# Spreading the shift products of an adaptive-norm attention kernel, with its first input tracked in token halves

## The chip, the cores and the metric

The kernel runs on one core of one Trainium2 chip. The metric is the device time of one execution in microseconds (us), median of several runs. For each run the span of the core's work (about 1.8 us less than the time, in most runs) and the mean granted TensorE clock are known too.

## The reference, cut to what matters

```
mod = silu(c) @ w_mod -> sa, ca, ga, sb, cb, gb          # six rows of 1024
h   = layernorm(x) * (1 + ca) + sa                       # x: 2048 x 1024
q   = h @ wq                                             # 32 heads of 128
p   = softmax(q @ k.T / sqrt(128)); o = p @ v            # 512 keys, 4 key groups
x   = x + ga * (o @ wo)
h   = layernorm(x) * (1 + cb) + sb
x   = x + gb * ((silu(h @ w_gate) * (h @ w_up)) @ w_down)
```

All in bf16 with f32 accumulation. The change touches only the start: the first `h`, the first eight heads of `q` for tokens 0 to 511, and the first iterations of attention.

## The kernel before

Tokens go in chunks of 512. The kernel does not wait for the shift `sa`: it projects the first eight heads from the scaled input alone ("raw" queries), and adds the shift's contribution, `sa @ wq`, later, as a column of 128 numbers a head. These columns are the *shift products*: 8 matmuls of one column for each head. `T.op` records who reads and writes each buffer and sets the semaphore waits; a buffer is one record, whatever part of it is used. `PB[b]` is the record of PSUM bank `b`.

```python
def x_gain(hf):                      # gain columns 1 + ca, four at a time
    V.tensor_copy(mod_bf[:, jt:jt + HK], psap(XB * 512, [[2, HK]]))      # PSUM -> bf16
    mod_gain(0, hf * HK, HK, B_modc, B_g[0])                             # + 1, bf16
    A.activation(gain_f[...], gain[0][...], AF.Copy)                     # f32 copy for ACT

def x_mod(hf, c0, n):                # scale tokens c0 .. c0+n of four chunks of the input
    for dt in (0, 2, 1, 3):
        ...                          # DVE for chunks 0, 1; ACT for chunks 2, 3
        ... writes=[PB[dt // 2], B_hT[0][dt]]      # one record for both token halves

for kc in range(HK):                 # first token half, heads 0 to 2
    for h in range(3):
        q_first(h, kc, 0, 2 * P)     # reads B_hT[0][kc]
    if kc == 2:
        x_first(tl, 0, HK)           # transposes of tile 3
        x_mod(0, 2 * P, 2 * P)       # second token half
        norm_last(512, 512)
for k in range(4): mod_ca(1, k)
for kc in range(HK):
    for h in range(3): q_first(h, kc, 2 * P, 2 * P)
x_first(2, HK, HK); x_first(tl, HK, HK)
for k in range(4, DT): mod_ca(1, k)
x_gain(1); x_mod(1, 0, CH)
...
def q_bias_mm(h0, h1):               # shift products of heads h0 .. h1-1
    for h in range(h0, h1):
        for kc in range(DT):
            mm(bank(BB, 1, 2 * h), wq_s[sl][...], mod_bf[:, kc:kc + 1], ..., PB[BB])  # BB = SCB + 3
    V.tensor_copy(bq[:, h0:h1], psap(BB * 512 + 2 * h0, ...))
...
for i in range(1, NA + 2):           # one attention head an iteration
    if i % 4 == 1 and i > 1: load_wq((i + 3) // 4 + 1)   # 1 MB of query weights
    if 2 <= i < NQ0: q_shifted(i)
    ...
    if i in LOADO: load_wo(LOADO[i])                     # 1 MB of output weights
    if 2 <= i < 1 + Hkv:
        k_turn(i - 1, XB); V.tensor_copy(kd, ks)         # one key group through bank XB
    ...
    if i == 1: scores(0); q_bias_mm(2, NQ0)              # 48 products
    if i > NQ0: qproj(i + LEAD)
    elif i % 2 == 0: qproj(NQ0 - 1 + i // 2)             # heads 8, 9, 10 at i = 2, 4, 6
    ...
    if 1 <= i - 1 < NA: scores(i - 1)
    if 0 <= i - 2 < NA: pv(i - 2)
```

The loads that matter here are all issued by one engine (SP), in program order: ..., query weights of group 2, the second token chunk of `x` (1 MB), keys of groups 1 to 3, values.

The softmax here doesn't subtract the row's maximum and nothing guards it: scores larger than these inputs give would overflow.

## Time and profile before

| | value |
|---|---|
| median of the three runs known at the start | 1278.52 us (1278.47 to 1280.67) |
| the profiled run: time, span, mean granted clock | 1281.05 us, 1279.3 us, 0.997 |
| PE busy; chain of waits on PE | 99%; 98% |

These are the page's busy line and the chain line of the kernel before. PE is the whole story: a gain has to come out of PE's gaps or its clock.

```profile
PE 1262.2 (99%) x7542; PEld 646.7 (51%) x7684; DVE 479.9 (38%) x896; ACT 341.8 (27%) x390; POOL 42.0 (3%) x102
...
PE 98%; issue 1%; ACT 0%; DVE 0%; POOL 0%; POOLq 0%; ACTq 0%
```

The next lines are from the timeline of PE in the kernel before: start, duration, line, operation, output and input, count, and in brackets PE's idle time before it with what ended it. Line 268 is the helper that issues every matmul, 272 the one for transposes; `128x1` are the one-column products.

```profile
start us, us, engine line op out<-in xcount [idle before <-releaser]
...
13.75 0.50 PE L268 MATMUL ps<-arena 128*128 128x256 bf16 x3 [1.07 <-ACT arena L492]
...
18.03 5.34 PE L268 MATMUL ps<-arena 128*128 128x512 bf16 x24 [0.35 <-DVE arena L489]
...
33.67 1.42 PE L268 MATMUL ps<-mod_bf,arena 128*128 128x1 bf16 x48 [1.80 <-ACT arena L755]
34.95 0.59 PE L272 MATMUL ps<-arena 128*128 128x128 bf16 x4
35.76 5.89 PE L268 MATMUL ps<-arena 128*128 128x512 bf16 x27 [0.22 <-DVE bq L663]
```

Three things are to be seen. At 13.75 PE had waited 1.07 us for a write by ACT. At 33.67 it had waited 1.80 us for ACT's exponentials, for the 48 shift products write a bank that the scores also use. And the stretch of 27 matmuls that begins with head 8's projection, at 35.76, took 5.89 us, far too long for its work. The windows view of the same kernel tells why: the third number from the end of a line, after the engines' busy times, is the clock granted to PE (here 0.89, 0.50, 0.93).

```profile
core 0: us, PE busy (x) PEld busy (x) DVE busy (x) ACT busy (x) POOL busy (x), PEclk, DMA share, GB/s
30.00:35.00 5.00, 3.14 (x57) 1.80 (x56) 3.14 (x11) 2.64 (x3) 0.00 (x0) 0.89 1.06 303
35.00:40.00 5.00, 4.78 (x18) 1.99 (x16) 1.68 (x4) 0.16 (x1) 0.00 (x0) 0.50 0.15 57
40.00:45.00 5.00, 4.95 (x51) 3.43 (x51) 2.80 (x8) 3.93 (x4) 0.00 (x0) 0.93 0.13 26
```

### The profile page before, as it was taken

The page shows a single profiled execution, that of the slowest core. Times are in us where ns is not written, and L with a number is a line of the kernel's source. Part 1 is how long each engine was busy: PE and PEld are TensorE (multiplying, and loading weights), DVE is VectorE, ACT ScalarE, POOL GpSimd, SP SyncE. Part 2 cuts the span into 40 slices and gives each one's busy share as a digit, 9 for nine tenths or more (in the row PEclk, how much of TensorE's full clock was granted, in tenths as well). Part 3 has the DMA queues.
Part 4 walks back from the last instruction along what each step waited for, and adds up shares of the span by engine and source line. Part 5 has one row for each costly group of instructions (what it writes and reads, how often), then busy time and mean ns, then how long its engine had stood idle before and what let it go on. Part 6 is the DMA issues. An engine that isn't in the chain of part 4 may idle for free.

```text
span 1279.3 us, 17804 instructions
## 1 busy us (share of the span) xinstructions
PE 1262.2 (99%) x7542; PEld 646.7 (51%) x7684; DVE 479.9 (38%) x896; ACT 341.8 (27%) x390; POOL 42.0 (3%) x102
## 2 busy tenths in 40 slices
PE   8999999999999999999999999999999999999999
PEld 4565545655445664455654444444444444444444
DVE  4555324765237652265322321233222331221222
ACT  3555303555015550055520111011100111011100
POOL 1021000000000010000000000000000000000000
PEclk9899999999999999999999999999999999999999
DMA  9799402967008841054352974046421654035200
GB/s 325 202 237 263 104 1 68 203 138 161 9 19 179 163 104 42 1 128 116 71 148 75 282 236 132 18 146 166 134 73 41 199 147 132 17 115 165 66 9 25
DMA packets 235854, 155.31 MB, mean 121 GB/s; under 512 B 129024, under 2 KB 222080, under 8 KB 235776
## 3 DMA queue, kind: packets, MB, share of 16 engines
q1 hardware_dynamic: 177520, 95.45, 31.2%
q10 hardware_dynamic: 58256, 58.73, 14.5%
q8 instruction: 60, 0.98, 0.3%
q14 instruction: 18, 0.15, 0.0%
HBM read 119.54 MB, written 4.19 MB: 97 GB/s over the span
## 4 chain that ended last, share of the span: by engine, by line
PE 98%; issue 1%; ACT 0%; DVE 0%; POOL 0%; POOLq 0%; ACTq 0%
PE ps L268 98%; ACT arena L755 0%; PE ps L272 0%; ACT arena L492 0%; DVE arena L489 0%; DVE rl L773 0%; DVE arena L668 0%; POOL arena L296 0%; DVE tmp L795 0%; DVE arena L797 0%; DVE gain L462 0%; DVE mod_bf L477 0%; DVE bq L663 0%; POOL arena L291 0%; POOL arena L290 0%
## 5 line engine op out<-in xcount | busy, mean ns | idle before, releaser
L268 PE MATMUL ps<-arena 128*128 128x512 bf16 (+2 forms) x7237 | 1254.2, 333 | 12.3 <-POOL arena L407 2.2
L268 PEld LDWEIGHTS ps<-arena 128*128 128x128 bf16 x7379 | 636.3, 98 | 623.4 <-issue 5.5
L755 ACT ACTIVATE arena<-ps 128x1024 bf16<-128x1024 f32 x256 | 261.8, 1023 | 354.5 <-PE ps L268 342.7
L986 ACT ACTIVATE arena<-ps 128x512 bf16<-128x512 f32 x112 | 66.9, 597 | 506.4 <-PE ps L268 506.4
L987 DVE TENSOR_TENSOR arena<-ps,arena 128x512 bf16<-128x512 f32 x112 | 77.4, 691 | 276.3 <-PE ps L268 276.3
L795 DVE TENSOR_TENSOR tmp<-ps,rowb 128x512 f32<-128x512 f32 (+1 forms) x65 | 44.4, 683 | 319.1 <-PE ps L268 319.1
L642 DVE CAST arena<-ps 128x512 bf16<-128x512 f32 x120 | 83.0, 691 | 54.9 <-PE ps L268 54.9
L776 DVE TENSOR_TENSOR arena<-ps,rl 128x512 bf16<-128x512 f32 x128 | 88.5, 691 | 4.8 <-DVE rl L773 0.4
L773 DVE RECIPROCAL rl<-ps 128x4 f32<-128x4 f32 x128 | 23.3, 182 | 119.2 <-PE ps L268 119.2
L414 DVE BATCH_NORM_STATS2 st<-x_res 128x6 f32<-128x512 bf16 x62 | 42.3, 683 | 3.5 <-DMA x_res<-in_A_x_dram 3.4
L419 POOL TENSOR_SCALAR rstd<-mv 128x1 f32<-128x1 f32 x28 | 6.3, 226 | 893.8 <-DVE mv L418 893.8
L587 DVE SCALAR_TENSOR_TENSOR arena<-arena 128x1024 bf16<-128x1024 bf16 x24 | 29.2, 1215 | 0.0
L797 DVE TENSOR_TENSOR arena<-tmp,x_res 128x512 bf16<-128x512 f32 (+1 forms) x33 | 22.3, 676 | 1.1
L797 DVE TENSOR_TENSOR x_res<-tmp,x_res 128x512 bf16<-128x512 f32 x32 | 22.1, 692 | 1.1
L430 DVE TENSOR_SCALAR arena<-arena,gain,mod_bf 128x512 bf16<-128x512 bf16 x56 | 20.3, 405 | 0.0
L425 DVE TENSOR_SCALAR nsc<-x_res,mv,rstd 128x1024 bf16<-128x1024 bf16 x30 | 16.0, 534 | 0.0
L421 POOL TENSOR_TENSOR rstd<-rstd,mhalf 128x1 f32<-128x1 f32 x28 | 15.8, 563 | 2.3
L602 POOL TENSOR_SCALAR arena<-arena,c 128x128 bf16<-128x128 bf16 x24 | 14.4, 616 | 32.7 <-PE ps L268 32.4
L268 PEld LDWEIGHTS ps<-sc_bf,arena 128*128 128x128 bf16 x192 | 6.7, 96 | 2.3
L268 PE MATMUL ps<-sc_bf,arena 128*128 128x1 bf16 x192 | 6.8, 163 | 0.1
L418 DVE BATCH_NORM_AGGREGATE mv<-st 128x2 f32<-128x12 f32 x28 | 5.8, 209 | 1.0
L655 DVE COPY arena<-ps 128x512 f32<-128x512 f32 x4 | 2.7, 689 | 7.9 <-PE ps L268 7.9
(53 smaller groups left out, 50.9 us busy)
## 6 DMA issues: line engine op xcount, KB each, us to landing
arena<-in_A_wq_dram SPq DMA_DIRECT2D x31, 1024.0 KB, 6.0
arena<-in_B_w_gate_dram ACTq DMA_DIRECT2D x28, 1024.0 KB, 5.4
arena<-in_B_w_up_dram ACTq DMA_DIRECT2D x28, 1024.0 KB, 8.3
arena<-in_A_wo_dram SPq DMA_DIRECT2D x8, 1024.0 KB, 7.8
arena<-in_B_w_down_dram SPq DMA_DIRECT2D x7, 1024.0 KB, 8.5
out_dram<-arena SPq DMA_DIRECT2D x15, 256.0 KB, 2.0
x_res<-in_A_x_dram SPq DMA_DIRECT2D x3, 1024.0 KB, 7.8
arena<-in_w_mod_dram SPq DMA_DIRECT2D x8, 256.0 KB, 6.0
```

The source lines that it names most:

```text
L268: T.op(PE, lambda: TE.matmul(out_ap, lhsT, rhs, start=start, stop=stop, skip_group_check=skip), reads=reads, writes=[bank_buf])
L414: T.op(DVE, lambda: V.bn_stats(st_[sl][:, hf * 6:hf * 6 + 6], x_res[:, t, hf * 512:hf * 512 + 512]), reads=[B_x[t]], writes=[B_st[sl]])
L430: T.op(DVE, lambda: V.tensor_scalar(dst[:, dt, :], dst[:, dt, :], gain[gi][:, dt:dt + 1], mod_bf[:, ccol + dt:ccol + dt + 1], op0=ALU.mult ...
L587: T.op(DVE, lambda: V.scalar_tensor_tensor(mt[n % 2], mt[n % 2], 1.0, sc_row, op0=ALU.mult, op1=ALU.mult, accum_out=mcol[:, n:n + 1]), rea ...
L642: T.op(DVE, lambda: V.tensor_copy(qT_s[qs], bank(b)), writes=[PB[b], B_qT[qs]])
L755: T.op(ACT, lambda: A.activation(ex_s[es][:, 2 * kp:2 * kp + 2, :], banks2(SCB + 2 * kp), AF.Exp, scale=att_scale), writes=[PB[SCB + 2 * k ...
L773: T.op(DVE, lambda: V.reciprocal(rl[r][:, :].rearrange("p (a b) -> p a b", a=2), psap(PVB * 512 + P, [[512, 2], [130, 2]])), writes=both + ...
L776: T.op(DVE, lambda: V.tensor_tensor(o_s[os_].rearrange("p (a b) d -> p a b d", a=2), psap(PVB * 512, [[512, 2], [130, 2], [1, P]]), rlb, A ...
L795: T.op(DVE, lambda: V.tensor_tensor(tmp[s][:, 0:n], bank(b, n), rowb[ri][:, c0:c0 + n], ALU.mult), reads=[B_row[ri]], writes=[PB[b], B_tmp ...
L797: T.op(DVE, lambda: V.tensor_tensor(dst[:, c0:c0 + n], tmp[s][:, 0:n], x_res[:, t, c0:c0 + n], ALU.add), reads=[B_tmp[s], B_x[t]], writes= ...
L986: T.op(ACT, lambda: A.activation(sg_s[ss], bank(gb), AF.Silu), writes=[PB[gb], B_sg[ss]])
L987: T.op(DVE, lambda: V.tensor_tensor(guT[:, ft, :], bank(ub), sg_s[ss], ALU.mult), reads=[B_sg[ss]], writes=[PB[ub], B_gu[ft]])
```

## The change

The intent is to start the first projections and head 8's projection earlier: (1) the two token halves of the first input get records of their own, and the second gain columns are prepared sooner; (2) the gain is read from PSUM once, as f32, for both engines; one warm-up matmul goes; (3) the shift products are made 16 at a time in iterations one, three and five, into the query bank, which nothing else uses then; (4) key groups 2 and 3 are both turned in iteration three; (5) the load of the query weights of heads 12 to 15 moves from iteration five to six, since their slot is read by the last shift products. Cut to its core:

```diff
 def x_gain(hf):
-    tensor_copy(mod_bf[...], psap(XB * 512, [[2, HK]])); mod_gain(0, ...)
-    A.activation(gain_f[...], gain[0][...], AF.Copy)
+    V.tensor_scalar(gain_f[:, hf * HK:(hf + 1) * HK], psap(XB * 512, [[2, HK]]), 1.0, None, op0=ALU.add)
-def x_mod(hf, c0, n):                       # ... writes B_hT[0][dt]
+def x_mod(hf, c0, n, bufs):                 # ... writes bufs[dt]
 ...
-                if k % 2 == 1:
+                if k == 5:
                     warm(1, WB)
 ...
-                    x_mod(0, 2 * P, 2 * P)
+                    x_mod(0, 2 * P, 2 * P, B_hB)
 ...
+            x_first(2, HK, HK)
             for kc in range(HK):
                 for h in range(3):
-                    q_first(h, kc, 2 * P, 2 * P)
-            x_first(2, HK, HK)
-            x_first(tl, HK, HK)
-            for k in range(4, DT):
-                mod_ca(1, k)
-            x_gain(1)
-            x_mod(1, 0, CH)
+                    q_first(h, kc, 2 * P, 2 * P, B_hB)
+                if kc == 1:
+                    x_first(tl, HK, HK)
+                    for k in range(4, DT):
+                        mod_ca(1, k)
+                    x_gain(1)
+                    x_mod(1, 0, CH, B_hT[0])
 ...
-                if i % 4 == 1 and i > 1:
+                if i % 4 == 1 and i > 5 or i == 6:
                     load_wq((i + 3) // 4 + 1)
 ...
-                if 2 <= i < 1 + Hkv:
-                    k_turn(i - 1, XB)
+                for gk in {2: (1,), 3: (2, 3)}.get(i, ()):
+                    k_turn(gk, XB)
 ...
                     if i == 1:
                         scores(0)
-                        q_bias_mm(2, NQ0)
+                    if i in (1, 3, 5):
+                        q_bias_mm(i + 1, i + 3, QB)
```

More of the change, by code (lines that the diff above doesn't have):

```diff
@@ L458, in mod_mm, with mod_gain @@
                        k == 0 and n == 0, k == DT - 1, [wbuf, B_sc], PB[XB], skip=True)
-            def mod_gain(gi, d0, n, cbuf, gbuf):
-                jt = (1 + 3 * gi) * DT + d0
-                T.op(DVE, lambda: V.tensor_scalar(gain[gi][:, d0:d0 + n], mod_bf[:, jt:jt + n], 1.0, None, op0=ALU.add),
+            def mod_gain(gi, cbuf, gbuf):
+                jt = (1 + 3 * gi) * DT
+                T.op(DVE, lambda: V.tensor_scalar(gain[gi][:, :], mod_bf[:, jt:jt + DT], 1.0, None, op0=ALU.add),
                      reads=[cbuf], writes=[gbuf])
@@ L475, in x_gain @@
             def x_gain(hf):
-                jt = DT + hf * HK
-                T.op(DVE, lambda: V.tensor_copy(mod_bf[:, jt:jt + HK], psap(XB * 512, [[2, HK]])), writes=[PB[XB], B_modc])
-                mod_gain(0, hf * HK, HK, B_modc, B_g[0])
-                T.op(ACT, lambda: A.activation(gain_f[:, hf * HK:(hf + 1) * HK], gain[0][:, hf * HK:(hf + 1) * HK], AF.Copy),
-                     reads=[B_g[0]], writes=[B_gf])
-            def x_mod(hf, c0, n):
+                T.op(DVE, lambda: V.tensor_scalar(gain_f[:, hf * HK:(hf + 1) * HK], psap(XB * 512, [[2, HK]]), 1.0, None, op0=ALU.add),
+                     writes=[PB[XB], B_g[0]])
+            def x_mod(hf, c0, n, bufs):
                 for dt in (0, 2, 1, 3):
@@ L488, in x_mod @@
                     if dt % 4 < 2:
-                        T.op(DVE, lambda: V.tensor_scalar(dst, src, gain[0][:, dt:dt + 1], None, op0=ALU.mult),
-                             reads=[B_g[0]], writes=[PB[dt // 2], B_hT[0][dt]])
+                        T.op(DVE, lambda: V.tensor_scalar(dst, src, gain_f[:, dt:dt + 1], None, op0=ALU.mult),
+                             reads=[B_g[0]], writes=[PB[dt // 2], bufs[dt]])
                     else:
                         T.op(ACT, lambda: A.activation(dst, src, AF.Copy, scale=gain_f[:, dt:dt + 1]),
-                             reads=[B_gf], writes=[PB[dt // 2], B_hT[0][dt]])
+                             reads=[B_g[0]], writes=[PB[dt // 2], bufs[dt]])
             MCOLS = [(j, j) for j in range(DT)]
@@ L553, in _ @@
             x_gain(0)
-            x_mod(0, 0, 2 * P)
+            x_mod(0, 0, 2 * P, B_hT[0])
             norm_last(0, 512)
@@ L655, in q_raw, with q_bias_mm @@
                     T.op(DVE, lambda: V.tensor_copy(qf[h], bank(QB0[h])), writes=[PB[QB0[h]], B_qf[h]])
-            def q_bias_mm(h0, h1):
+            def q_bias_mm(h0, h1, BB):
                 for h in range(h0, h1):
@@ L685, in k_evac, with q_first @@
                 return (kT_sb[:, gk * KT:(gk + 1) * KT, :], bank_bf(b)[:, 0:KT * P].rearrange("p (a b) -> p a b", a=KT))
-            def q_first(h, kc, c0, n):
+            B_hB = [_Buf("hB%d" % dt) for dt in range(DT)]
+            def q_first(h, kc, c0, n, bufs=B_hT[0]):
                 mm(bank(QB0[h], n, c0), wq_s[0][:, kc, h * P:(h + 1) * P], hT[0][:, kc, c0:c0 + n],
-                   kc == 0 and c0 == 0, kc == DT - 1, [B_wq[0][kc // HK], B_hT[0][kc]], PB[QB0[h]], skip=True)
+                   kc == 0 and c0 == 0, kc == DT - 1, [B_wq[0][kc // HK], bufs[kc]], PB[QB0[h]], skip=True)
             for kc in range(HK):
@@ L716, in _ @@
                 q_raw(h)
+            T.op(DVE, lambda: V.tensor_copy(gain[0][:, :], gain_f[:, :]), writes=[B_g[0]])
             qproj_mm(4, QB0[4], 0, DT)
@@ L733, in _ @@
             qproj_mm(7, QB0[7], 0, HK)
-            q_bias_mm(0, 2)
+            q_bias_mm(0, 2, BB)
             q_shifted(0)
@@ L848, in _ @@
                     load_wo(LOADO[i])
-                if 2 <= i < 1 + Hkv:
-                    k_turn(i - 1, XB)
-                    kd, ks = k_evac(i - 1, XB)
-                    T.op(DVE, lambda: V.tensor_copy(kd, ks), writes=[PB[XB], B_kT[i - 1]])
-                    if i == Hkv:
+                for gk in {2: (1,), 3: (2, 3)}.get(i, ()):
+                    k_turn(gk, XB)
+                    kd, ks = k_evac(gk, XB)
+                    T.op(DVE, lambda: V.tensor_copy(kd, ks), writes=[PB[XB], B_kT[gk]])
+                    if gk == Hkv - 1:
                         for b_ in B_hT[1]:
@@ L887, in _ @@
                         if g0 == 1:
-                            mod_gain(1, 0, DT, B_late[2], B_g[1])
+                            mod_gain(1, B_late[2], B_g[1])
                         elif g0 == 2:
```

## The prediction

> **What bounds the kernel.** TensorE. The page gives PE 1262.2 us busy of a 1279.3 us span (99%), and the chain of waits is 98% PE. From 60 us to the end I find almost no PE wait, and the diff changes nothing there. All that can be won lies in the first 55 us, where the timeline shows four PE gaps: 10.75-11.3, 12.7-13.75, 17.7-18.03 and, largest, 31.9-33.67. So this is a change of a microsecond or two.
>
> **Front (to 21 us).** In the timeline PE waits 1.07 us, until 13.75, for an ACT write of the second token half (12.72 + 2 x 0.49): chunk 3 of the first half is held by a record shared by both halves. Separate records let it run at about 12.6. The second half's and tile 3's transposes and the gain columns then move up: the gain read, at 17.00 before, comes at about 15.15 (the last gain weights land at 14.1, the DMA view), one DVE op of 0.16 us instead of DVE 0.16 + DVE 0.17 + ACT 0.20 with gaps. Chunks 4 to 7 start at 16.6 rather than 18.03: 1.4 us gained. The weights they need land at 15.6 and 18.6, and the shift weights at 21.2, 0.3 us before their new use, so I expect no new wait. Dropping one warm matmul and the ACT copy of the gain before 11.3 gains nothing: there PE waits for query weights that land at 11.1-11.3.
>
> **Shift products.** Before, 48 one-column products (1.42 us) write a score bank and so wait 1.80 us for the two exponentials (ACT 31.47-33.61); the first full projection starts at 35.76. After, 16 products (0.48 us) go to the query bank without waiting. Then the transposes of key group 1 wait for keys that land at about 32.25 (issued 23.03, 9.2 us to landing), so the projection starts near 32.7: 3.1 us earlier in all. Part is given back: in iteration three two key groups turn through one bank, the second waiting for a DVE copy that queues behind reciprocal, scaling and a query shift (0.2 + 0.7 + 0.5 + 0.4 us). PE should stand about 1.3 us at 36.6-37.9, and 16 products follow (0.48). The last 16, in iteration five, fill the 0.46 us wait for ACT seen at 48.35, so cost nothing. Walked through in order with these durations, PE ends 1.3 us ahead at iteration six, and keeps that.
>
> **Clock.** The windows view shows a granted clock of 0.50 from 33.9 to 40.6 us: twelve 512-column matmuls start 0.43 us apart instead of 0.216, a loss of some 2.4 us. The Trainium skill (TensorE: Matmul & The Clock Gate, Part 1) says a free-running window of about 3.4 us of low activity halves the clock; this trace agrees (6.7 us, two windows). As the phase is free, not every run need pay: 1280.67 and the profiled 1281.05 against 1278.47 and 1278.52 differ by just that, so I take the median before to be an unpaid run. The new gaps (about 1.45 and 1.3 us) are shorter than 1.8 us, so I expect the half clock more rarely, perhaps never.
>
> **Time.** 1278.5 - 1.3 = 1277.2 us; range 1275.0 to 1279.0. Faster by over 2%: 0.005, within 2%: 0.99, slower: 0.005.
>
> **Would show it right.** The gain read at about 15.2; first projection after the scores at 32-33; PE wait for keys, then a wait of about 1.3 us for the DVE key copy; no wait at iteration five; clock 1.00 between 30 and 45 us; runs closer together.
>
> **Would make it wrong.** The new gaps trip the half clock (up to 2 us back); shift weights landing later than planned; the unpaid runs before were partly paid (then 1275 is possible).

## The result

| | before | after |
|---|---|---|
| median, runs | 1279.27 us, 4 (1278.47 to 1280.67) | 1280.25 us, 4 (1279.87 to 1281.39) |
| ratio after over before | | 1.0008, 95% interval 0.9991 to 1.0025 |
| profiled run: span, clock | 1279.3 us, 0.997 | 1277.5 us, 1.000 |

1280.25 us lies outside the predicted 1275.0 to 1279.0 and nothing of the 1.3 us is seen. (Three of the four runs after also have 2.3 us outside the span instead of the usual 1.8; that half microsecond lies outside the core's work.)

One trap lies in the table. The two profiled spans differ by 1.8 us in favour of the change, but the one before ran partly at half clock and the one after did not. They can't be compared as they stand.

The busy line and the chain line of the changed kernel, which answer to those of before: the chain is now 96% PE, the rest being SP's issues and two loads.

```profile
PE 1259.3 (99%) x7541; PEld 646.0 (51%) x7683; DVE 480.1 (38%) x897; ACT 341.8 (27%) x388; POOL 42.2 (3%) x102
...
PE 96%; SPq 2%; DMA 1%; issue 1%; DVE 0%; ACT 0%
```

PE's timeline in the changed kernel, columns as before:

```profile
12.86 0.49 PE L268 MATMUL ps<-arena 128*128 128x256 bf16 x3
...
15.09 6.86 PE L268 MATMUL ps<-arena 128*128 128x256 bf16 x33
...
30.29 0.54 PE L268 MATMUL ps<-mod_bf,arena 128*128 128x1 bf16 x16
33.07 0.40 PE L272 MATMUL ps<-arena 128*128 128x128 bf16 x4 [2.24 <-DMA arena<-in_A_k_cache_dram]
33.30 3.66 PE L268 MATMUL ps<-arena 128*128 128x512 bf16 x27
36.80 0.39 PE L272 MATMUL ps<-arena 128*128 128x128 bf16 x4
38.78 0.38 PE L272 MATMUL ps<-arena 128*128 128x128 bf16 x4 [1.59 <-DVE arena L853]
...
50.57 0.94 PE L268 MATMUL ps<-sc_bf,arena 128*128 128x1 bf16 x32
...
57.52 1.90 PE L268 MATMUL ps<-arena 128*128 128x512 bf16 x7 [0.71 <-DMA arena<-in_A_wq_dram]
59.25 0.34 PE L268 MATMUL ps<-sc_bf,arena 128*128 128x1 bf16 x8
```

The front went as predicted: no wait at 12.86, chunks 4 to 7 within the run of matmuls that starts at 15.09, the shift products at 30.29 unhindered. Then PE stands 2.24 us for the keys of group 1 and 1.59 us between the two key turns of iteration three, and, not predicted at all, 0.71 us for query weights at 57.52. (The lines at 50.57 and 59.25 serve as marks below.) The windows of the changed kernel show a full clock in this run:

```profile
30.00:35.00 5.00, 2.71 (x30) 1.57 (x29) 2.83 (x11) 2.05 (x2) 0.00 (x0) 1.00 0.99 262
35.00:40.00 5.00, 3.33 (x47) 2.45 (x47) 2.87 (x7) 2.05 (x2) 0.00 (x0) 1.00 0.45 148
40.00:45.00 5.00, 5.00 (x60) 3.42 (x59) 2.09 (x5) 3.43 (x4) 0.00 (x0) 1.00 0.79 238
```

The chain of waits of the changed kernel, from 18.94 us on (start, duration, what), names the owners of the three waits:

```profile
18.94 4.01 SPq L299
...
22.99 10.04 DMA arena<-in_A_k_cache_dram
...
37.00 0.19 DVE rl L774
...
37.22 0.69 DVE arena L777
37.91 0.39 DVE arena L665
38.30 0.34 DVE arena L853
...
49.51 7.96 DMA arena<-in_A_wq_dram
```

The keys (issued at 22.99) landed 10.04 us later, behind the 4.01 us issue of 1 MB of `x` (line 299). The copy that frees the bank (line 853) queued behind the reciprocal (774), the scaling (777) and a query shift (665). The query weights issued at 49.51 took 7.96 us.

### The profile page after: what moved, and what is told of

Its sections match the earlier page's. It is cut to its first block, busy times and chain, and to the rows that moved or that the text cites. A ratio compares the mean times of both kernels' runs of the same rounds, so it can differ in the third digit from the quotient of the medians.

```text
span 1277.5 us, 17800 instructions
## 1 busy us (share of the span) xinstructions
PE 1259.3 (99%) x7541; PEld 646.0 (51%) x7683; DVE 480.1 (38%) x897; ACT 341.8 (27%) x388; POOL 42.2 (3%) x102
## 4 chain that ended last, share of the span: by engine, by line
PE 96%; SPq 2%; DMA 1%; issue 1%; DVE 0%; ACT 0%
PE ps L268 96%; DMA arena<-in_A_k_cache_dram 1%; DMA arena<-in_A_wq_dram 1%; SPq L331 0%; SPq L299 0%; SPq L354 0%; SPq L384 0%; SPq L363 0%; SPq L306 0%; SPq L358 0%; ACT arena L756 0%; DVE rl L774 0%; PE ps L272 0%; SPq L389 0%; DVE arena L777 0%
## 5 line engine op out<-in xcount | busy, mean ns | idle before, releaser
L599 POOL TENSOR_SCALAR arena<-arena,c 128x128 bf16<-128x128 bf16 x24 | 14.4, 618 | 32.7 <-PE ps L268 32.4
L272 PE MATMUL ps<-arena 128*128 128x128 bf16 x32 | 3.1, 218 | 3.8 <-DMA arena<-in_A_k_cache_dram 2.2
```

## The experiments

**Theory A**: the three waits are new or newly bare, and each ate a part of the gain. **Theory B**: the half clock decides; both kernels have runs with and without it, and this hides or makes the difference. **Theory C** (for two runs): the front's gain is lost somewhere later in any case. In what follows "at full clock" means runs whose mean granted clock is shown as 1.000. All kernels gave correct results. The kernels came five rounds each, beside nine runs of the kernel before.

| kernel | spans at clock 1.000, us | spans below 1.000, us | median time (before) |
|---|---|---|---|
| before, 32 runs in all | 1276.7 to 1277.1 (16 runs) | 1278.0 to 1279.8 (16) | |
| changed, first job | 1277.5, 1277.7 | 1278.6, 1279.1 | 1280.25 (1279.27) |
| changed, again | 1276.4, 1276.6, 1277.2 | 1278.4, 1278.9 | 1279.09 (1278.66) |
| keys_early | 1276.2, 1276.6, 1276.6 | 1278.4, 1278.4 | 1278.47 (1278.66) |
| wq3_first | 1275.8, 1275.8 | 1277.4, 1277.6, 1277.7 | 1279.31 (1278.66) |
| turns_spread | 1275.9, 1275.9 | 1276.6, 1277.0, 1277.7 | 1278.49 (1278.66) |
| front_only | 1275.1, 1275.2, 1275.2, 1275.4 | 1276.5 | 1277.11 (1279.91) |
| bias_only | 1278.0, 1278.1, 1278.7 | 1279.8, 1279.8 | 1280.48 (1279.91) |
| before_filled | 1277.4, 1277.4, 1277.5, 1277.5, 1277.7 | none | 1279.28 (1279.91) |
| after_filled | 1277.4, 1277.9, 1278.3, 1278.8, 1279.0 | none | 1280.12 (1278.90) |
| front_filled | 1275.0, 1275.6, 1275.6, 1276.1, 1276.4 | none | 1278.04 (1278.90) |
| all_three | 1273.5, 1273.7, 1273.7, 1273.7, 1274.0 | none | 1275.57 (1278.90) |
| three_filled | 1273.4, 1273.4, 1273.6, 1273.6, 1274.3 | none | 1275.81 (1278.90) |

### after_again: the changed kernel, unedited

> The changed kernel again, unedited, for a baseline on this chip with more rounds. Theory A (new waits ate the gain: keys landing at 33.0 us, the second key turn's 1.6 us wait for a DVE copy, the 0.7 us wait for the query weights of heads 12 to 15 at 57.5 us): ratio to the kernel before 1.000 to 1.001, the same three PE waits within 0.3 us. Theory B (the half clock decides: runs of either kernel fall on two levels about 2 us apart, by the phase of the clock's window): a ratio that moves with how many runs of each show a clock below 1.000.

Measured: ratio 1.0001 (0.9989 to 1.0014); waits of 2.1, 1.6 and 0.8 us. At full clock its runs are within half a microsecond of those of before, so the gain is missing at full clock as well: theory B can't be the whole cause. But two of five runs fall to the lower level, as three of the nine of before do, so the change does not spare the half clock either.

### before_again: the kernel before, against itself

> The kernel before against itself, for the spread and, if its profile falls at a clock of 1.000, for its own walk through the first 60 us without the half clock. Expected: ratio 1.000 within 0.001; spans of 1276.7 to 1277.1 at clock 1.000, of 1278.5 to 1279.8 below it; at full clock head 8's projection starts at 35.5 to 35.8 us and iteration seven's gate products at 50.7 to 50.9.

Measured: ratio 0.9996, three of five runs at full clock, the profiled one among them, so its timeline is the fair counterpart of the changed kernel's:

```profile
33.71 1.35 PE L268 MATMUL ps<-mod_bf,arena 128*128 128x1 bf16 x48 [1.80 <-ACT arena L755]
34.93 0.38 PE L272 MATMUL ps<-arena 128*128 128x128 bf16 x4
35.36 3.44 PE L268 MATMUL ps<-arena 128*128 128x512 bf16 x27
...
50.67 0.94 PE L268 MATMUL ps<-sc_bf,arena 128*128 128x1 bf16 x32
...
58.47 0.34 PE L268 MATMUL ps<-sc_bf,arena 128*128 128x1 bf16 x8
```

The same wait of 1.80 us is there, without the half clock. Head 8's projection starts at 35.36 (a little before the 35.5 to 35.8 that I expected), not at 35.76, and its stretch of 27 matmuls takes 3.44 us, not 5.89: the half clock cost 2.45 us there. It had also slowed the products and the key turn before that by 0.4 us, which the prediction booked as gain of the change. 50.67 and 58.47 (the gate products of iterations seven and nine) serve as marks below.

### front_only and bias_only: each half of the change alone

```diff
 # front_only: parts 1 and 2 of the change; products, key turns, loads as before
 # bias_only: parts 3, 4 and 5; the front as before
```

> The kernel before with the front part of the change alone (split records of the token halves, gain columns read once, one warm matmul less); shift products, key turns and weight loads as before. Theory A (the two parts don't add: the keys' landing at 33 us takes what the front saved): here the keys are not asked for until after the 48 products, at about 33.7 us, so the front's 1.4 us passes whole: span at clock 1.000 of 1275.2 to 1275.7 against 1276.75. Rival C (the front's gain is lost somewhere later in any case, for instance at the query weights): 1276.4 to 1276.9.

Measured: 1275.1 to 1275.4 us at full clock, 1.6 us less than before, ratio 0.9982 (0.9968 to 0.9996). PE's timeline of front_only shows the gain arriving whole: the projection at 33.72 instead of 35.36, the mark at 49.03 instead of 50.67.

```profile
33.72 3.44 PE L268 MATMUL ps<-arena 128*128 128x512 bf16 x27
...
49.03 0.94 PE L268 MATMUL ps<-sc_bf,arena 128*128 128x1 bf16 x32
```

> The kernel before with the shift products, key turns and weight load of the change, without its front part. Theory A: head 8's projection starts at 33.4 to 33.7 us, just where the whole change has it, though the front is 1.4 us later, for the keys decide; span at clock 1.000 of 1276.4 to 1277.0, as the whole change. Rival C: 1.4 us later than the whole change, 1277.8 to 1278.4.

Measured: 1278.0 to 1278.7 us at full clock, 1.5 us *more* than before by their means, ratio 1.0007. PE's timeline of bias_only:

```profile
32.43 0.40 PE L272 MATMUL ps<-arena 128*128 128x128 bf16 x4
33.65 3.66 PE L268 MATMUL ps<-arena 128*128 128x512 bf16 x27 [0.82 <-DVE bq L663]
...
39.12 0.38 PE L272 MATMUL ps<-arena 128*128 128x128 bf16 x4 [1.59 <-DVE arena L852]
...
58.01 1.90 PE L268 MATMUL ps<-arena 128*128 128x512 bf16 x7 [0.87 <-DMA arena<-in_A_wq_dram]
```

The projection starts at 33.65, when theory A said, but not for its reason; that is close to the changed kernel's 33.30 (32.95 in its second profile). So of the front's 1.6 us only 0.35 to 0.7 us is left by then when both parts are there. In this kernel the keys are not waited for (the turn at 32.43 follows the products at once); the shift copy is; theory A's figure for the start was met by luck. With the front part PE comes early enough to hit the keys. The span I expected for bias_only was too low, since some of the front does get through; and 1.5 us worse than before means that parts 3 to 5 alone give back more than they gain: the projection starts 1.7 us earlier; but from there to the mark of iteration seven (50.91 here) PE takes 17.26 us instead of 15.31, with 1.59 us between the turns and 32 products that are still to be made, and from there to the mark of iteration nine (59.75) 8.84 us instead of 7.80, with 0.87 us for query weights. That makes 1.3 us in all, the difference of the two profiled spans (1278.0 and 1276.7). Theory C's figure for that span fits, but not its reason, for front_only kept all of its gain.

### keys_early: keys ahead of the second token chunk

```diff
             load_wq(2)
-            load_x(1)
             for gk in range(1, Hkv):
                 load_k(gk)
+            load_x(1)
```

> The changed kernel with the keys of groups 1 to 3 asked for ahead of the 1 MB of the second token chunk. Theory A: keys 1 land near 30 us, the PE wait of 2.2 us for them shrinks to about 0.8 us (then the shift products' copy at 31.9 us holds the query bank), qproj of head 8 starts at 31.9 to 32.2 us rather than 33.5, and 1.2 to 1.5 us of it reach the end: 0.999 of the changed kernel. Theory B: no change of the time beyond the shift of clock levels, or a changed share of runs at a clock below 1.000.

Measured: the wait for keys is gone and the projection starts at 32.00, as expected; but at full clock the spans are 1276.2 to 1276.6, a gain of 0.3 us and not 1.2 to 1.5. The list of PE's waits (total, times, longest) shows what remained:

```profile
PE ps L272 <- DVE arena L853: 1.6, 1, 1.6
PE ps L268 <- DMA arena<-in_A_wq_dram: 1.2, 1, 1.2
PE ps L268 <- DVE bq L660: 1.0, 1, 1.0
```

Of the 2.1 to 2.2 us for the keys, 1.0 us was handed to the next wait, that for the copy of the shift columns (line 660). The wait for query weights is 1.2 us now, where it was 0.7 to 0.8, but not because PE comes sooner. In all six profiles that load these weights in iteration six behind the output weights, the load is issued 1.06 or 1.07 us before the mark of iteration seven: it moves with PE. Here it took 8.5 us to land instead of 8.0; why is open. (This profile ran at half clock from about 38.5 to 41.9 us, one window, after a gap of 1.60 us.) By the profiles, the projection is 0.95 to 1.3 us earlier and half a microsecond is lost to the longer landing, which leaves 0.45 to 0.8 us. The profiled run of after_again, at 1277.2 us, is 0.6 to 1.0 us above these three spans; the mean gain is only 0.3 us because the two other full-clock runs of after_again, which have no profile, were faster.

### wq3_first: query weights of heads 12 to 15 ahead of the first output weights

```diff
-                if i % 4 == 1 and i > 5 or i == 6:
+                if i % 4 == 1 and i > 5:
                     load_wq((i + 3) // 4 + 1)
-                if i in LOADO:
+                if i in LOADO and i > 5:
 ...
                         q_bias_mm(i + 1, i + 3, QB)
+                        if i == 5: load_wq(3); load_wo(0)
```

> The changed kernel with the query weights of heads 12 to 15 asked for in iteration five right behind the last shift products, ahead of the first 1 MB of output weights, in place of iteration six. Theory A: issued near 47 us rather than 49.5, the weights are there in time, the PE wait of 0.7 us at 57.5 us goes, and 0.7 us reaches the end. Theory B: within 0.3 us of the changed kernel at equal clock.

Measured: 1275.8 us at full clock, 0.9 us less than the changed kernel's mean, and the wait at 57.5 is gone. How it came about is seen in SP's timeline, first of the kernel before, at full clock (line 354 is a load of query weights, 789 one of output weights):

```profile
47.21 0.52 SPq L354 DMA_DIRECT2D arena<-in_A_wq_dram  x1
47.77 0.58 SPq L789 DMA_DIRECT2D arena<-in_A_wo_dram  x1
```

and then of the changed kernel (790 is the load of output weights, 780 the transposes of attention outputs):

```profile
47.04 0.58 SPq L790 DMA_DIRECT2D arena<-in_A_wo_dram  x1
48.21 1.19 SPq L780 DMA_TRANSPOSE arena<-arena  x1
49.51 0.52 SPq L354 DMA_DIRECT2D arena<-in_A_wq_dram  x1
```

Moved by one iteration, the load changed places with 1 MB of output weights and with a transpose: issued 2.3 us later, it also took 8.0 us to land instead of 5.4. In wq3_first it is issued at 48.13 and lands in 5.5 us, though that profiled run lost time to the half clock.

### turns_spread: one key turn an iteration again

```diff
-                for gk in {2: (1,), 3: (2, 3)}.get(i, ()):
+                for gk in {2: (1,), 3: (2,), 4: (3,)}.get(i, ()):
```

> The changed kernel with the key turns of groups 2 and 3 in iterations three and four again, as before. Theory A: the PE wait of 1.6 us at 37.2 to 38.8 us goes; about 0.4 us of it comes back as the wait for the exponentials' banks and 0.4 us as the turn in iteration four, so 0.8 to 1.2 us less at iteration six, but the wait for the query weights at 57.5 us then grows by about as much, since their issue waits on the copies rather than on PE, so the end moves by 0 to 0.8 us. Theory B: the removed gap leaves fewer runs at a clock below 1.000, nothing else.

Measured: the wait of 1.6 us is gone, the query-weight wait is 0.9 us, and the span at full clock is 1275.9, 0.8 us less, at the upper end of what was expected. PE's timeline of turns_spread:

```profile
33.25 3.66 PE L268 MATMUL ps<-arena 128*128 128x512 bf16 x27
...
48.77 0.94 PE L268 MATMUL ps<-sc_bf,arena 128*128 128x1 bf16 x32
```

From the projection to the mark PE takes 15.52 us, against 17.27 in both profiles of the changed kernel. That the wait for query weights would then grow by about as much was wrong: it is 0.15 to 0.2 us longer, for their load is issued at 47.71 instead of 49.16 or 49.51, 1.06 us before the mark as ever. Three of five runs still fell below 1.000, so removing this gap alone does not avoid the half clock.

### before_filled, after_filled and front_filled: the half clock taken away

Matmuls on zeros go into a bank that is free at the time; nothing reads their result, and no wait is removed. (`warm(n, b)` is the kernel's own warm-up helper.)

```diff
 # before_filled and front_filled
                         scores(0)
+                        warm(8, PVB + 1)
                         q_bias_mm(2, NQ0)
 # after_filled
+                if i == 2: warm(9, PVB + 1)              # before the first key turn
                 for gk in {2: (1,), 3: (2, 3)}.get(i, ()):
+                    if gk == 3: warm(6, QB)              # between the two turns
```

> The kernel before with 8 matmuls on zeros into a free bank while PE waits for the first head's exponentials (1.73 us of work in a gap of 1.8 us). Theory B (the half clock, called by the low activity at 31.9 to 35.8 us, makes the two levels of the runs): the windows have 1.00 throughout, no run of the five lies over 1277.3 us of span, the median is that of the fast level, 1276.7 to 1276.9. If the levels have another cause, one to three of the five lie at 1278.5 or more.

> The changed kernel with matmuls on zeros in its two long gaps: 9 while PE waits for the keys, 6 between the two turns of iteration three. Waits and work stay as they are. Theory B: clock 1.000 in all runs, spans 1276.4 to 1277.8 in a narrow band, so no gain over the fast runs of either kernel; what the change lost at full clock is still lost. Were the half clock all that ate the gain, the spans would be 1275.5 or less.

> front_only with the 8 matmuls on zeros of before_filled in the wait for the first head's exponentials. Theories A and B together: front_only's span at full clock, 1275.1 to 1275.9, in all five runs, clock 1.000; against before_filled 1.6 to 2.2 us less.

Measured: all fifteen runs are at clock 1.000, against sixteen of thirty-two for the kernel before and five of nine for the changed one. before_filled's five spans lie within 0.3 us, where before spreads over 3.1 us. So the gaps do make the two levels, and theory B is right about them. It is not right about the missing gain: after_filled is no faster than the fast runs of before.

The levels themselves came out higher than I expected in before_filled and after_filled, and in two of the five runs of front_filled. before_filled lies 0.7 us above the fast runs of before. In its profile the twelve warm-up matmuls at 3.24 us took 5.03 us, against 3.99 in before_again, and everything from there on is 0.5 us late; why all five runs should be so is open. after_filled and front_filled spread over 1.6 and 1.4 us at full clock. Their profiled runs have a wait of 0.6 and 0.8 us near 657 us for a transpose of attention outputs, far from anything edited, which the other profiles do not show. Without it these two spans would be about 1277.3 and 1275.3, an estimate from 1277.9 and 1276.1 and within what I expected. I have no cause for it.

### all_three and three_filled: the three edits together

```diff
 # all_three = keys_early + wq3_first + turns_spread
 # three_filled, in addition, after the key turn of iteration two:
+                    if gk == 1: warm(4, PVB + 1)
```

> The changed kernel with all three edits: keys asked for ahead of the second token chunk, the query weights of heads 12 to 15 in iteration five ahead of the first output weights, one key turn an iteration. Theory A (the three waits are worth their lengths): none of the three PE waits is left, head 8's projection starts at 31.9 to 32.2 us, span at clock 1.000 of 1273.5 to 1274.5 against 1276.7 to 1276.8 of the kernel before; some runs still fall to a clock below 1.000, 0.7 to 2 us above. If the waits only move on, a new PE wait of over 0.5 us stands in the list and the span is 1275 or more.

> As all_three, with 4 matmuls on zeros into a free bank in the one gap left (0.9 us, before head 8's projection). Theory B in its narrow form[...]: no run below a clock of 1.000, runs within 0.6 us of each other, median time 1275.4 to 1276.4. This is the version that should beat both kernels, and front_only.

Measured: all_three runs in 1275.57 us, ratio to before 0.9970 (0.9957 to 0.9982), spans 1273.5 to 1274.0, by the means 3.2 us under the full-clock runs of before. PE's timeline of all_three:

```profile
32.07 3.66 PE L268 MATMUL ps<-arena 128*128 128x512 bf16 x27 [0.99 <-DVE bq L660]
...
47.59 0.94 PE L268 MATMUL ps<-sc_bf,arena 128*128 128x1 bf16 x32
...
55.39 0.34 PE L268 MATMUL ps<-sc_bf,arena 128*128 128x1 bf16 x8
```

One wait of 0.99 us is left, for the copy of the shift columns. Alone the three edits gave 0.3, 0.9 and 0.8 us, together 3.0 us, each against the changed kernel's full-clock mean of 1276.7 (all_three ran in another call). That the sum of the three is smaller does not show that the edits need one another: these are means of two to five runs, and the changed kernel's own full-clock spans lie up to 0.8 us apart in one call. On PE's timelines the parts add up. The projection starts at 32.00 in keys_early and at 32.07 here, instead of 32.95 or 33.30. From there to the mark of iteration seven it is 15.52 us in turns_spread and here, instead of 17.27. From there to the mark of iteration nine it is 7.80 us in wq3_first and here, instead of 8.74 or 8.68. Together that is 3.6 or 3.9 us, and the profiled spans differ by 3.5 or 3.8 (1273.7 against 1277.2 and 1277.5). No run of all_three fell to the lower level, which I had expected of some; so three_filled, equal within its spread, proves nothing about its filler here. Both beat the two kernels, by some 0.3%, and all_three is 1.5 us better than front_only at full clock, as far as runs of two calls can be compared.

## Why the prediction was wrong

The class (within 2%) was right and could hardly fail. The median, 1280.25 us, was above the range, and the predicted gain of 1.3 us was not there.

- **Front: right.** Predicted 1.4 us, 1.6 us in front_only. PE's times in the changed kernel (12.86, the gain read at 15.44, no wait for the shift weights) are as foretold.
- **The step that failed** is "Walked through in order with these durations, PE ends 1.3 us ahead at iteration six, and keeps that." At the mark of iteration seven the changed kernel is 0.1 to 0.45 us ahead of before at full clock (50.57 and 50.22 against 50.67), and at that of iteration nine it is 0.5 to 0.8 us *behind* (58.96 and 59.25 against 58.47). Its terms:
  - *Start of head 8's projection before*, taken as 35.76 from a profile at half clock; 35.36 at full clock. 0.4 us of gain that never was. I set the half clock apart in the prediction, and still took a mark from inside it.
  - *Keys land at "about 32.25"*: PE took them at 33.07 and 32.72, and the projection began at 33.30 and 32.95 instead of 32.7. 0.25 to 0.6 us. I took the landing of one profile for a constant. The Trainium skill (DMA: Bandwidth & Descriptors, Queues, rings and completion order) says that descriptors on each DMA engine are consumed in ring order; the trace agrees, for the keys landed at 33.0 us, just after the 1 MB of `x` issued ahead of them (18.94, 13.7 us to landing), and at 29.0 us, in time, once that was put behind them.
  - *Wait between the key turns*: predicted 1.3, measured 1.59 us. 0.3 us.
  - *Query weights of heads 12 to 15*: not in the prediction at all; 0.71 and 0.77 us. I read the moved load as a safe reordering, since four iterations were left, and did not ask what it would queue behind. It was issued 1.06 us before the mark of iteration seven instead of 3.46, and took 8.0 us to land instead of 5.4.
  - These sum to 1.65 to 2.1 us against 1.3 us, which is 0.35 to 0.8 us behind; the second mark says 0.5 to 0.8.
- **Clock: half right.** Before has two levels, as inferred, and filling the gap removes the lower one. But "I expect the half clock more rarely, perhaps never" failed: four of nine runs of the changed kernel have it. Its gaps are 2.24 and 1.59 us rather than 1.45 and 1.3, so the argument from shorter gaps fell with the two mis-sized waits.
- **Last products in iteration five free: right.** PE's list of waits has none there, and the 32 products of iterations three and five together add only 0.21 us between projection and mark in turns_spread (15.52 against 15.31).

That 1280.25 is above the changed kernel's later medians is due in part to half of those four runs being at the lower level and, in three, to half a microsecond outside the span. Why its full-clock spans were 1277.5 and 1277.7 in that job and 1276.4 to 1277.2 in the next stays open; between the two profiled runs the keys' landing (PE took them at 33.07 and 32.72) makes the 0.3 us.

## What to carry to other kernels

When a change lets an engine run ahead, look up what lands and what comes free at the new time, not at the old one. Ask of each load whether its issue moves with that engine, as that of the query weights did here, or not, as that of the keys: only the second kind takes away what was won before it. A removed wait can feed another, as the keys' fed that for the shift columns. Stretches between marks on one engine's timeline tell what each part costs where the means of a few runs do not. A load moved by one iteration may change places with a megabyte in the queue. Before comparing two profiles for a microsecond, see that their clocks are equal, and sort the timed runs by clock first.

## What the Trainium skill lacked or had wrong

- *TensorE: Matmul & The Clock Gate*: Part 1 states a free-running window of about 3.4 us, and the closing table asks for no idle gaps over about 3 us between bursts of matmuls. The window agrees: half clock for 3.4 us in keys_early and for 6.7 us in the profile before. The gap does not: with 1.80 us of idle PE, followed by one-column products, 16 of 32 runs had a clock below 1.000 (none of five with the gap filled), and in keys_early a gap of 1.60 us preceded the half clock. About half a window idle was enough in these runs, while all_three, whose longest gap past 12 us is 0.99 us, kept 1.000 in five of five. The page gives no figure below 3 us.
- The same page tells that the warm-up at the start differs from run to run. It does not tell that a gap in mid-kernel then splits the runs of one program into two levels, here 1276.7 to 1277.1 and 1278.0 to 1279.8 us of span, which a few runs' median may take for a change of the kernel; nor that filler matmuls on zeros in the gap end it (15 of 15 runs at full clock).
- *DMA: Bandwidth & Descriptors* gives the ring order but no page warns what it does to small loads: 128 KB of keys took 9.0 to 10.2 us from issue to landing behind 1 MB of other data.
